# Holding five more chunks over into the next stage three of a long-convolution kernel

## The chip, the cores and the metric

The kernel runs on one core of one Trainium2 chip. The metric is the device time of one execution in microseconds (us): 1001.87 us before the change, median of 3 runs (998.74 to 1006.28).

## The reference

For a batch of 8 sequences of 6400 positions and 128 channels, the reference makes a causal long convolution and then a small gated layer:

```python
y = np.fft.irfft(np.fft.rfft(x, n=2*S, axis=1) * np.fft.rfft(h, n=2*S, axis=0)[None], n=2*S, axis=1)[:, :S]
gate_pre[:, s] = sum(conv_w[k] * y[:, s - 4 + k] for k in range(5))     # causal, 5 taps, per channel
gate = 1 / (1 + np.exp(-gate_pre))
out = (gate * (y @ w_val)) @ w_out
```

## The kernel before, in words

A position is n1 * 64 + n2, with 100 values of n1 and 64 of n2. The long convolution is done by two-step transforms, all as float32 matmuls. **Stage one** (`Forward`) transforms over n1: 16 steps of 32 short matmuls, fed by `sums`, in which GpSimd (POOL) writes the sum and the difference of the two halves of x into one of three buffers `sd`. **Stage two** (`s2_mm`, `Product`) transforms over n2 in 13 blocks `kb`: 16 matmuls `pt<-gy,m` with matrices from a ring of three buffers `m2_sb`, two multiplications on VectorE (DVE) with the filter's spectrum from a ring of four buffers `h_sb`, and two additions on GpSimd. **Stage three** (`s3_quads`) transforms back over k2 in 16 steps of 64 short matmuls `pt<-r_sb,gy`. **Stage four** (`Chunk.s4`) transforms back over k1: 20 matmuls `pt<-m_sb,dt` for a chunk of five n2; the 13 chunks are `HEAD` (60 to 63) and those that begin at 0, 5, ... 55.

The gated layer works on these chunks. `copies` puts the chunk from PSUM into `y` and starts the taps on ScalarE (ACT); `taps` adds three products per chunk on DVE (`more`, a read-modify-write of the running sum in "cells" of n2) and a fourth on GpSimd, which adds a buffer `p` that ACT had scaled. Tap j of the chunk at a adds into cells a+j to a+j+4, so neighbouring chunks write the same cells. Then come `project` (y times w_val, four matmuls of 500 columns), `sigm` on ACT, `gate` on DVE, `output` (four matmuls), and `store`.

The eight sequences b run in one software pipeline of two stretches per sequence, and every engine works strictly in the order of the program text. The **stage-three stretch** runs stage three of b with stage one of b+1, step by step: `s3_quads`, then `half` of the next sequence, then `sums` for a later `half`, then the leftover work that `steps[g]` lists. The **stage-four stretch** runs stage four of b, one chunk per step s, with stage two of b+1, one block per step. In it a chunk's taps come at step s+1, its projection at s+2, its output matmuls at s+3. For the five chunks 35 to 55 ("late") only `y` is kept; their taps, projections and outputs are left over to the next stage-three stretch, since they have storage of their own (`yl`, `gl`). The others keep `y` and cells inside `dt`, which the next stage three overwrites. The last sequence (b = 7) has no stage one or two beside it and no late chunks.

PSUM has two pairs of banks (`pair`, stages two and three) and four single banks (`single`: stage one's halves, `s4`, `project`, `output`).

Of the kernel before, what the change touches and what calls it, by code (L numbers as in the profile page):

```python
# [10 lines left out]
F32 = mybir.dt.float32  # L11
# [5 lines left out]
C = 128  # L17
N1 = 100
N2 = 64
# [5 lines left out]
SB = 4  # L25
NKB = 13
TAPS = 5
XG = 4
NS = C // (2 * XG)
NW = 2 * C + TAPS  # L30
CH = 5
HEAD = (60, 4)
# [1 line left out]
NCH = len(CHUNKS)  # L34
OUT_ORDER = CHUNKS[1:] + [HEAD]
LATE = 35
DEFER = 35
M2B = 3
MH = 6
HB = 4  # L40
XB = 3
XH = 8


def _out_range(ch):
# [76 lines left out]
def longconv_moe(ctx: ExitStack, tc: tile.TileContext, x, h, r1, m2, r3, m4, w64, out):  # L122
    nc = _Engines(tc)
    B = x.shape[0]
    MUL, ADD = ALU.mult, ALU.add

    cp = ctx.enter_context(tc.tile_pool(name="cp", bufs=1))
# [9 lines left out]
    dv = dt.rearrange("p (n c d) -> p n c d", c=2, d=C)  # L137
# [5 lines left out]
    wc_sb = w_sb[:, 2 * C :]  # L143
    gl = cp.tile([128, N2 - LATE, N1], F32, name="gl")
    yl = {a: cp.tile([128, n, N1], F32, name=f"yl_{a}") for a, n in CHUNKS if a >= LATE}
    m2_sb = [cp.tile([128, SB, 2, C], F32, name=f"m2_{i}") for i in range(M2B)]
    h_sb = [cp.tile([128, 2 * SB * C], F32, name=f"h_{i}") for i in range(HB)]
    x_sb = [cp.tile([128, 2, XG, N2], F32, name=f"x_{i}") for i in range(XB)]
    sd_sb = [cp.tile([128, 2, XG, N2], F32, name=f"sd_{i}") for i in range(3)]
    p_t = [cp.tile([128, CH, N1], F32, name=f"p_{i}") for i in range(2)]  # L150
# [118 lines left out]
    def count(kb):  # L269
        return min(SB, HR - kb * SB)  # L270
# [122 lines left out]
    def cells(x, n):  # L393

        out, i = [], 0
        while i < n:
            y = x + i
            end = 4 if y < 4 else LATE if y < LATE else N2
            k = min(n - i, end - y)
            s = (y - 4) % N2  # L400
            out.append((i, gl[:, y - LATE : y - LATE + k] if y >= LATE else dv[:, s : s + k, 1, :N1]))
            i += k
        return out

    class Chunk:


        def __init__(self, b, ch, defer):
            self.b, self.ch = b, ch
            a, n = ch  # L410
            self.late = defer and DEFER <= a < HEAD[0]
            self.y = yl[a][:, :n] if a >= LATE else dv[:, a : a + n, 0, :N1]

        def s4(self):
            a, n = self.ch
# [23 lines left out]
        def copies(self):  # L439
            a, n = self.ch  # L440
            if a == HEAD[0]:
                for i, o in cells(0, n):
                    nc.gpsimd.memset(o[:, :, :1], 0.0)
                    self.first(4, o[:, :, 1:], self.p[:, i : i + n, : N1 - 1])
                act(self.y, self.p)
                for i, o in cells(a, n):
                    self.first(0, o, self.p)
            else:
                act(self.y, self.p)
                if not self.late:  # L450
                    self.init()
                    self.q = p_t[a // CH % 2]
                    self.first(3, self.q, self.p)
            if self.late:
                self.p = self.y

        def init(self):
            a, n = self.ch
            for i, o in cells(a + 4, min(n, HEAD[0] - a - 4)):
                self.first(4, o, self.p[:, i : i + o.shape[1]])  # L460

        def taps(self, js=range(4)):
            a, n = self.ch
            if self.late and 0 in js:
                self.init()
                self.q = p_t[a // CH % 2]
                self.first(3, self.q, self.p)
            if a == HEAD[0]:
                for j in range(1, 4):
                    for i, o in cells(a + j, n - j):  # L470
                        self.more(j, o, self.p[:, : n - j])
                    for i, o in cells(0, j):
                        self.more(j, o[:, :, 1:], self.p[:, n - j :, : N1 - 1])
                return
            k = HEAD[0] - a - 4
            if k < n and 0 in js:
                for i, o in cells(HEAD[0], n - k):
                    self.more(4, o, self.p[:, k:])
            for j in js:
                if j < 3:  # L480
                    for i, o in cells(a + j, n):
                        self.more(j, o, self.p[:, i : i + o.shape[1]])
            if 3 not in js:
                return
            for i, o in cells(a + 3, n):
                nc.gpsimd.tensor_tensor(out=o, in0=o, in1=self.q[:, i : i + o.shape[1]], op=ADD)

        def project(self):
            n = self.ch[1]
# [37 lines left out]
        )  # L527
        for i in range(XH - XB)
    ]
# [7 lines left out]
    for g, (f, i) in enumerate(order):  # L537
        e = f.half()
# [12 lines left out]
        a = slice(CH * j, CH * j + CH + (j == 12))  # L551
        nc.sync.dma_start(m4_sb[:, a], m4.rearrange("k (n t) -> k n t", t=MW)[:, a])

    m4_rest = [12, 11, 10, 9, 4, 8, 5, 7, 6]
    sp, pr = {0: Spectrum(0)}, {}
    for kb in range(-1, NKB + 1):
        if 0 <= kb < NKB:
# [20 lines left out]
    pend = []  # L578
    for b in range(B):
        nxt = b + 1 < B  # L580


        steps = collections.defaultdict(list)
        for m, c in enumerate(pend[1:]):
            steps[2 * m] += [lambda c=c: c.taps(range(2))]
            steps[2 * m + 1] += [lambda c=c: c.taps(range(2, 4))]
            steps[2 * m + 2] += [c.project, c.sigm, c.gate]
            if m < 3:
                steps[2 * m + 4] += [c.output]
                steps[2 * m + 5] += [c.store]  # L590
        if pend:
            steps[13] += [pend[0].project, pend[0].sigm, pend[0].gate]
        if nxt:
            for _ in range(2):
                fx.sums(nc.gpsimd)
        for g in range(NS):
            e = s3_quads(4 * g)
            f = []
            if nxt:
                f = fx.half([single(), single()])  # L600
                fx.sums(nc.gpsimd)
            for u in e:
                u()
            for u in f:
                u(act)
            if b == 0:
                next(wgen, None)
                next(wgen, None)
                if g % 3 == 0 and g < 12:
                    m4_load(m4_rest.pop(0))  # L610
            if nxt and g % 2 and g > 1:
                kb = g // 2 - 1
                if kb < M2B:
                    m2_load(kb)
                elif kb < M2B + HB - 1:
                    h_load(kb - M2B)
            for u in steps[g]:
                u()
        if nxt:
            h_load(HB - 1)  # L620
        if b + 2 < B:
            fx = Forward(x[b + 2], gy)


        cs = [Chunk(b, ch, nxt) for ch in CHUNKS]
        jobs = collections.defaultdict(list)
        for i, c in enumerate(cs):
            if i and not c.late:
                jobs[i + 2 if nxt else (5, 6, 7, 8, 9, 10, 11, 11, 12, 13, 13, 14)[i - 1]].append(c)
        if not nxt:  # L630
            jobs[NCH + 1].append(cs[0])
        ps, outs = {}, []
        for s in range(max(NCH - 1, *jobs) + 2):
            if s < 2:
                cs[s].s4()
            if s == 0 and pend:
                pend[0].output()
                pend[0].store(p_t[1][:, : HEAD[1]])
            if nxt and s == 0:
                ps[0] = Product(0)  # L640
                m2_load(M2B)
            if nxt and s + 1 < NKB:
                ps[s + 1] = Product(s + 1)
                m2_load(s + 1 + M2B)
# [6 lines left out]
            late = pend[4 + s : 5 + s] if s < 2 else []  # L651
            for c in outs + late:
                c.output()
            for c in jobs[s]:
                c.sigm()
            if s < NCH:
                cs[s].copies()
            for c in outs + late:
                c.store()
            if s in ps:  # L660
                ps[s].mul_u()
                ps[s].mul_t()
                ps.pop(s).add()
                h_load(s + HB)
# [7 lines left out]
        pend = [cs[0]] + [c for c in cs if c.late]  # L672


def _lay_x(v):
# [42 lines left out]
```

## Time and profile before

| | |
|---|---|
| runs | 1006.28, 1001.87, 998.74 us; median 1001.87 |
| profiled execution | 1004.56 us, of which the span from the first to the last instruction is 1002.7 |
| busy share of the span | PE 87%, PEld 72%, DVE 74%, POOL 57%, ACT 51% |
| granted TensorE clock | 0.954 (mean) |
| stretches | start 97.6 us; seven cycles of a stage-three stretch (53.1 to 56.5 us) and a stage-four stretch (57.8 to 60.8 us); last sequence 42.6 and 60.4 us |
| DMA | 177.40 MB, mean 177 GB/s |

How it is read: PE is TensorE's matmuls, PEld its weight loads, which run beside them, SP the queue that issues DMAs. "Busy" is the time in which an engine has an instruction in work; `x40` is a number of instructions; the part in brackets is the idle time before, and who ended it. Every instruction bears the line of one helper (L109), so groups are told apart by their tiles: `out<-in`. A window's bounds are microseconds from the span's start.

### The profile page before, as it was taken

Reading aid. Unit: us, or ns where it says so; the run is one execution under the profiler, and the core shown is the slowest. Engines: PE = TensorE matmul, PEld = TensorE weight load, DVE = VectorE, ACT = ScalarE, POOL = GpSimd, SP = SyncE. Lnnn points to the kernel's source line nnn. Section 1 sums busy time; section 2 is a strip of 40 time slices with the busy share of each in tenths; the row PEclk is TensorE's granted clock in tenths of the full one; section 3 lists DMA queues with packets and bytes.
Section 4 is the critical chain, followed back from the end, with each engine's and each line's share of the span. In section 5 each row is a group of like instructions: output and inputs, shape, how many; then the busy total and the mean of one; then the engine's idle time right before and its main releaser. Section 6 shows DMA issues by size and latency. Waiting matters only on the chain. (4 is left out here: it accounts for less than half of the span.)

```text
span 1002.7 us, 47817 instructions
## 1 busy us (share of the span) xinstructions
PE 871.8 (87%) x21360; PEld 719.6 (72%) x21360; DVE 745.1 (74%) x1033; ACT 509.6 (51%) x1207; POOL 570.1 (57%) x586
## 2 busy tenths in 40 slices
PE   7898769988799879988899778988799888997778
PEld 6798668775688558775788657876688757884554
DVE  5556547968598767968499675968589675978666
ACT  4431444546553654547444663546544574545456
POOL 5457535775477754786277663776367762761032
PEclk9799879999999989999899999999899999999999
DMA  7684647846486456855486565855478454850103
GB/s 255 229 304 190 192 141 258 262 107 185 154 264 185 144 160 213 231 135 164 142 264 183 141 197 162 242 157 162 134 240 222 139 170 138 266 144 23 42 22 111
DMA packets 96844, 177.40 MB, mean 177 GB/s; under 512 B 43392, under 2 KB 49792, under 8 KB 96640
## 3 DMA queue, kind: packets, MB, share of 16 engines
q1 hardware_dynamic: 96640, 174.35, 56.2%
q8 instruction: 168, 2.75, 1.1%
q14 instruction: 36, 0.29, 0.1%
HBM read 141.56 MB, written 32.77 MB: 174 GB/s over the span
## 5 line engine op out<-in xcount | busy, mean ns | idle before, releaser
L109 POOL TENSOR_TENSOR gy<-gy,h 128x512 f32<-128x512 f32 (+1 forms) x182 | 221.2, 1242 | 120.1 <-PE pt L109 87.5
L109 PEld LDWEIGHTS pt<-r_sb,gy 64*64 64x64 f32 x8192 | 157.1, 145 | 103.6 <-issue 60.6
L109 DVE TENSOR_TENSOR dt<-pt,h 128x496 f32<-128x496 f32 x256 | 159.7, 664 | 96.2 <-ACT dt L109 91.8
L109 PEld LDWEIGHTS pt<-m_sb,dt 128*64 128x64 f32 x4096 | 194.0, 139 | 51.2 <-issue 34.2
L109 PE MATMUL pt<-r_sb,gy 64*64 64x64 f32 x8192 | 173.6, 233 | 60.1 <-issue 45.2
L109 PE MATMUL pt<-m_sb,dt 128*64 128x100 f32 x4096 | 200.2, 253 | 14.5 <-DVE dt L109 13.0
L109 POOL TENSOR_TENSOR sd<-x 128x256 f32<-128x256 f32 x236 | 182.0, 803 | 47.1 <-issue 21.2
L109 PEld LDWEIGHTS pt<-gy,m 128*64 128x64 f32 x3008 | 179.8, 135 | 27.7 <-issue 22.8
L109 PE MATMUL pt<-r_sb,sd 50*64 50x100 f32 x4608 | 155.0, 270 | 46.0 <-issue 21.0
L109 PE MATMUL pt<-gy,m 128*64 128x128 f32 x3008 | 190.8, 277 | 0.6 <-PE pt L109 0.5
L109 PEld LDWEIGHTS pt<-r_sb,sd 50*64 50x64 f32 x4608 | 128.6, 149 | 55.1 <-issue 24.2
L109 ACT COPY dt<-pt 128x16 f32<-128x16 f32 (+3 forms) x397 | 113.8, 329 | 103.6 <-PE pt L109 103.6
L109 DVE TENSOR_TENSOR gy<-pt,h 128x1024 f32<-128x1024 f32 (+1 forms) x99 | 116.7, 1179 | 58.3 <-ACT gl L109 34.4
L109 DVE SCALAR_TENSOR_TENSOR dt<-pt,w_sb,dt 128x500 f32<-128x500 f32 (+7 forms) x216 | 132.5, 629 | 10.6 <-POOL dt L109 6.7
L109 ACT COPY gy<-pt 128x400 f32<-128x400 f32 x248 | 112.2, 512 | 42.5 <-PE pt L109 31.2
L109 ACT COPY h<-pt 128x512 f32<-128x512 f32 (+1 forms) x136 | 83.5, 614 | 91.5 <-issue 43.0
L109 POOL TENSOR_TENSOR gl<-gl,p 128x500 f32<-128x500 f32 (+1 forms) x48 | 56.8, 1183 | 114.4 <-DVE gl L109 94.0
L109 PE MATMUL pt<-dt,w_sb 128*64 128x500 f32 (+2 forms) x480 | 115.1, 555 | 2.4 <-ACT dt L109 1.8
L109 DVE SCALAR_TENSOR_TENSOR gl<-yl,w_sb,gl 128x500 f32<-128x500 f32 (+1 forms) x112 | 106.1, 953 | 13.4 <-ACT gl L109 12.1
L109 DVE TENSOR_TENSOR h<-pt,h 128x1024 f32<-128x1024 f32 (+1 forms) x91 | 107.7, 1183 | 3.1
L109 ACT COPY yl<-pt 128x500 f32<-128x500 f32 (+1 forms) x89 | 51.3, 577 | 91.8 <-PE pt L109 91.7
L109 POOL TENSOR_TENSOR dt<-dt,p 128x500 f32<-128x500 f32 (+1 forms) x64 | 66.3, 1041 | 23.2 <-PE pt L109 13.2
(44 smaller groups left out, 657.6 us busy)
## 6 DMA issues: line engine op xcount, KB each, us to landing
m<-m SPq DMA_DIRECT2D x90, 512.0 KB, 5.4
h<-hd SPq DMA_DIRECT2D x84, 512.0 KB, 5.1
x<-xl SPq DMA_DIRECT2D x118, 256.0 KB, 2.9
out<-dt SPq DMA_DIRECT2D x56, 250.0 KB, 4.4
out<-yl SPq DMA_DIRECT2D x40, 250.0 KB, 4.6
m_sb<-m SPq DMA_DIRECT2D x12, 375.0 KB, 5.9
hd<-h SPq DMA_DIRECT2D x8, 512.0 KB, 4.9
m_sb<-m SPq DMA_DIRECT2D x6, 512.0 KB, 7.2
```

Of the source, the lines that this page charges most:

```text
L109: return self._tc.keep_in_program_order(call(*args, **kwargs))
```

## The change

Five more chunks, those at 10, 15, 20, 25 and 30, are now "held" over into the next stage-three stretch, unless it is the last sequence.

- The seven buffers of `m2_sb` and `h_sb` become slices of one tile `ring`. When stage two is through with them, five slices take the held chunks' cells (`held_c`) and `y` (`held_y`).
- In the stage-four stretch the chunks come in another order: HEAD, 0, then the late 35 to 55, then 5, then the held 10 to 30. Stage two runs ahead: two blocks in an even step, one in an odd one, so that its 13 blocks end at step 8.
- The held chunks have their taps in the stage-four stretch still, but with tap 2 scaled by ACT into an `sd` buffer and added by GpSimd behind tap 3, where DVE had added it. Their projection, sigmoid and gate stand in steps 0 to 4 of the next stage-three stretch, output and store two and three steps later. The late chunks' leftover work moves from steps 0 to 10 to steps 4 to 14; four of their outputs, not three, now fit into the stretch.
- The loads of the next stage two's first blocks move to the steps in `AHEAD`, where a slice has come free. The last sequence projects each chunk two steps after its `s4`, and the last nine loads of `m4` are reordered for the new order of the chunks.

```diff
+HELD = 10
+AHEAD = {2: (1, 0), 7: (0, 0), 9: (0, 1), 10: (0, 2), 11: (1, 1), 13: (1, 2)}
...
-    m2_sb = [cp.tile([128, SB, 2, C], F32, name=f"m2_{i}") for i in range(M2B)]
-    h_sb = [cp.tile([128, 2 * SB * C], F32, name=f"h_{i}") for i in range(HB)]
+    ring = cp.tile([128, (M2B + HB) * BL], F32, name="ring")
+    held_c = ring[:, : (LATE - HELD) * N1].rearrange("p (n t) -> p n t", t=N1)
...
+        def keep(self):
+            i = self.ch[0] // CH % 2
+            self.q = {3: p_t[i]}
+            if self.held:
+                self.q[2] = sd_sb[i].rearrange("p a d n -> p (a d n)")[:, : CH * N1].rearrange("p (n t) -> p n t", t=N1)
+            for j, q in self.q.items():
+                self.first(j, q, self.p)
...
             for j in js:
-                if j < 3:
+                if j < 3 and j not in self.q:
                     for i, o in cells(a + j, n):
                         self.more(j, o, self.p[:, i : i + o.shape[1]])
...
-            for i, o in cells(a + 3, n):
-                nc.gpsimd.tensor_tensor(out=o, in0=o, in1=self.q[:, i : i + o.shape[1]], op=ADD)
+            for j, q in self.q.items():
+                for i, o in cells(a + j, n):
+                    nc.gpsimd.tensor_tensor(out=o, in0=o, in1=q[:, i : i + o.shape[1]], op=ADD)
...
+            elif c.held:
+                t = (a - HELD) // CH
+            else:
+                t = 6 + 2 * (a - LATE) // CH
+                steps[t - 2] += [lambda c=c: c.taps(range(2))]
+                steps[t - 1] += [lambda c=c: c.taps(range(2, 4))]
+            steps[t] += [c.project, c.sigm, c.gate]
+            if t + 2 < NS:
+                steps[t + 2] += [c.output]
+                steps[t + 3] += [c.store]
...
+        if nxt:
+            cs = cs[:2] + [c for c in cs if c.late] + [c for c in cs[2:] if not c.late]
         for i, c in enumerate(cs):
-            if i and not c.late:
-                jobs[i + 2 if nxt else (5, 6, 7, 8, 9, 10, 11, 11, 12, 13, 13, 14)[i - 1]].append(c)
+            if i and not c.late and not c.held:
+                jobs[i + 2].append(c)
...
         for s in range(max(NCH - 1, *jobs) + 2):
+            kbs = list(range(at, min(at + 2 - s % 2, NKB))) if nxt else []
+            at += len(kbs)
```

The rows that follow are the engines' instructions in program order around the seam between a stage-four and the next stage-three stretch. On GpSimd before (`gy<-gy,h` are stage two's additions, `dt<-dt,p` and `gl<-gl,p` the fourth tap, `sd<-x` the sums for the next `half`):

```order
L109 TENSOR_TENSOR dt<-dt,p_93 128x2x100
L109 TENSOR_TENSOR gl<-gl,p_93 128x300
L109 TENSOR_TENSOR gy<-gy,h_84 128x64x8 x2
L109 TENSOR_TENSOR gy<-gy,h_85 128x64x8 x2
L109 TENSOR_TENSOR gy<-gy,h_86 128x64x8 x2
L109 TENSOR_TENSOR gy<-gy,h_83 128x64x4 x2
L109 TENSOR_TENSOR sd_90<-x_87 128x256 x2
```

On GpSimd now (`ring<-ring,p` is tap 3 and `ring<-ring,sd` tap 2 of a held chunk; the two rows ahead of them are tap 3 of chunk 5):

```order
L111 TENSOR_TENSOR gy<-gy,ring 128x64x4 x2
L111 TENSOR_TENSOR dt<-dt,p_88 128x2x100
L111 TENSOR_TENSOR ring<-ring,p_88 128x300
L111 TENSOR_TENSOR ring<-ring,p_87 128x500
L111 TENSOR_TENSOR ring<-ring,sd_84 128x500
...
L111 TENSOR_TENSOR ring<-ring,p_87 128x200
L111 TENSOR_TENSOR gl<-gl,p_87 128x300
L111 TENSOR_TENSOR ring<-ring,sd_84 128x300
L111 TENSOR_TENSOR gl<-gl,sd_84 128x200
L111 TENSOR_TENSOR sd_84<-x_81 128x256 x2
```

The additions of stage two stood between the taps and the sums; now they are all ahead of the taps, and the tap additions of chunk 5 and of five held chunks (two full-size additions each, the last one in four pieces) stand directly ahead of the first sums. On DVE now, in the same place (`gy<-pt,ring` and `ring<-pt,ring` are stage two's multiplications of the last block, `dt<-pt,w_sb,dt` and `ring<-pt,w_sb,ring` are taps, `dt<-pt_2860,dt` is chunk 5's gate, the last row stage three's):

```order
L111 TENSOR_TENSOR gy<-pt_2786,ring 128x2x64x4
L111 TENSOR_TENSOR ring<-pt_2786,ring 128x512
L111 SCALAR_TENSOR_TENSOR dt<-pt_2795,w_sb,dt 128x5x100
...
L111 SCALAR_TENSOR_TENSOR ring<-pt_2795,w_sb,ring 128x200
L111 SCALAR_TENSOR_TENSOR ring<-pt_2824,w_sb,ring 128x500 x2
L111 TENSOR_TENSOR dt<-pt_2860,dt 128x5x100
L111 SCALAR_TENSOR_TENSOR ring<-pt_2863,w_sb,ring 128x500 x2
...
L111 SCALAR_TENSOR_TENSOR gl<-pt_2960,w_sb,gl 128x100
L111 TENSOR_TENSOR dt<-pt_3003,ring 128x124x4
```

Before, the last taps on DVE stood eight multiplications ahead of stage three's first instruction; now every multiplication of stage two is through before chunk 5's taps, and the taps of the held chunks follow one another with nothing but one gate between.

More of the change, by code (lines that the diff above doesn't have):

```diff
@@ L36 @@
 LATE = 35
-DEFER = 35
+HELD = 10
+BL = 2 * SB * C
 M2B = 3
@@ L145, in longconv_moe @@
     yl = {a: cp.tile([128, n, N1], F32, name=f"yl_{a}") for a, n in CHUNKS if a >= LATE}
-    m2_sb = [cp.tile([128, SB, 2, C], F32, name=f"m2_{i}") for i in range(M2B)]
-    h_sb = [cp.tile([128, 2 * SB * C], F32, name=f"h_{i}") for i in range(HB)]
+    ring = cp.tile([128, (M2B + HB) * BL], F32, name="ring")
+    ring_at = [ring[:, i * BL : (i + 1) * BL] for i in range(M2B + HB)]
+    m2_sb = [r.rearrange("p (s a c) -> p s a c", a=2, c=C) for r in ring_at[:M2B]]
+    h_sb = [ring_at[M2B + i] for i in (2, 0, 1, 3)]
+    held_c = ring[:, : (LATE - HELD) * N1].rearrange("p (n t) -> p n t", t=N1)
+    held_y = {
+        a: ring[:, i : i + CH * N1].rearrange("p (n t) -> p n t", t=N1)
+        for a, i in zip(range(HELD, LATE, CH), (2500, 3072, 3572, 4096, 4596))
+    }
     x_sb = [cp.tile([128, 2, XG, N2], F32, name=f"x_{i}") for i in range(XB)]
@@ L397, in cells @@
             y = x + i
-            end = 4 if y < 4 else LATE if y < LATE else N2
+            end = next(e for e in (4, HELD, LATE, N2) if y < e)
             k = min(n - i, end - y)
             s = (y - 4) % N2
-            out.append((i, gl[:, y - LATE : y - LATE + k] if y >= LATE else dv[:, s : s + k, 1, :N1]))
+            t, o = (gl, y - LATE) if y >= LATE else (held_c, y - HELD) if y >= HELD else (dv[:, :, 1, :N1], s)
+            out.append((i, t[:, o : o + k]))
             i += k
@@ L410, in __init__ @@
             a, n = ch
-            self.late = defer and DEFER <= a < HEAD[0]
-            self.y = yl[a][:, :n] if a >= LATE else dv[:, a : a + n, 0, :N1]
+            self.late = defer and LATE <= a < HEAD[0]
+            self.held = defer and HELD <= a < LATE
+            self.y = yl[a][:, :n] if a >= LATE else held_y[a] if a >= HELD else dv[:, a : a + n, 0, :N1]
         def s4(self):
@@ L451, in copies @@
                     self.init()
-                    self.q = p_t[a // CH % 2]
-                    self.first(3, self.q, self.p)
+                    self.keep()
             if self.late:
                 self.p = self.y
+        def keep(self):
[5 more added lines that the diff above has]
+                self.first(j, q, self.p)
         def init(self):
@@ L465, in taps @@
                 self.init()
-                self.q = p_t[a // CH % 2]
-                self.first(3, self.q, self.p)
+                self.keep()
             if a == HEAD[0]:
@@ L552, in m4_load @@
         nc.sync.dma_start(m4_sb[:, a], m4.rearrange("k (n t) -> k n t", t=MW)[:, a])
[L554 removed]
+    m4_rest = [12, 7, 5, 8, 4, 9, 10, 11, 6]
     sp, pr = {0: Spectrum(0)}, {}
@@ L583, in longconv_moe @@
         steps = collections.defaultdict(list)
[L584 to L592, printed above, removed]
+        for c in pend:
+            a = c.ch[0]
+            if a == HEAD[0]:
+                t = NS - 1
+            elif c.held:
[8 more added lines that the diff above has]
+                steps[t + 3] += [c.store]
+        pend = [c for c in pend if c.ch[0] in (HEAD[0], HEAD[0] - CH)]
         if nxt:
@@ L610, in longconv_moe @@
                     m4_load(m4_rest.pop(0))
[L611 to L616, printed above, removed]
+            if nxt and g in AHEAD:
+                f, kb = AHEAD[g]
+                (h_load if f else m2_load)(kb)
             for u in steps[g]:
@@ L625, in longconv_moe, with s2, times @@
         cs = [Chunk(b, ch, nxt) for ch in CHUNKS]
+        if nxt:
+            cs = cs[:2] + [c for c in cs if c.late] + [c for c in cs[2:] if not c.late]
         jobs = collections.defaultdict(list)
         for i, c in enumerate(cs):
-            if i and not c.late:
-                jobs[i + 2 if nxt else (5, 6, 7, 8, 9, 10, 11, 11, 12, 13, 13, 14)[i - 1]].append(c)
+            if i and not c.late and not c.held:
+                jobs[i + 2].append(c)
         if not nxt:
             jobs[NCH + 1].append(cs[0])
-        ps, outs = {}, []
+        pr = {}
+        def s2(kb):
+            if nxt and kb < NKB:
+                pr[kb] = Product(kb)
+                m2_load(kb + M2B)
+        def times(kb):
+            if kb in pr:
+                pr[kb].mul_u()
+                pr[kb].mul_t()
+                pr.pop(kb).add()
+                h_load(kb + HB)
+        outs, at = [], 0
         for s in range(max(NCH - 1, *jobs) + 2):
+            kbs = list(range(at, min(at + 2 - s % 2, NKB))) if nxt else []
+            at += len(kbs)
             if s < 2:
                 cs[s].s4()
[L636 to L644, printed above, removed]
+            late = pend[s : s + 1]
+            if late and s == 0:
+                late[0].output()
+                late[0].store(p_t[1][:, : HEAD[1]])
+                late = []
+            if s == 0:
+                s2(0)
+            for kb in kbs[:1]:
+                s2(kb + 1)
             if m4_rest:
@@ L650, in longconv_moe @@
                 cs[s].s4()
-            late = pend[4 + s : 5 + s] if s < 2 else []
             for c in outs + late:
@@ L655, in longconv_moe @@
                 c.sigm()
+            for kb in kbs[:1]:
+                times(kb)
+            for kb in kbs[1:]:
+                s2(kb + 1)
             if s < NCH:
@@ L659, in longconv_moe @@
                 c.store()
[L660 to L664, printed above, removed]
+            for kb in kbs[1:]:
+                times(kb)
             if 0 < s <= NCH and not cs[s - 1].late:
@@ L671, in longconv_moe @@
                 fx.load(XB)
-        pend = [cs[0]] + [c for c in cs if c.late]
+        pend = [cs[0]] + [c for c in cs if c.held or c.late]
 def _lay_x(v):
```

## The prediction

> **What bounds the kernel now.** I read the stretches first, with the busy time of each engine (length, then busy time and count of PE, PEld, DVE, ACT and POOL, granted clock, DMA share, GB/s).
>
> ```profile
> core 0: us, PE busy (x) PEld busy (x) DVE busy (x) ACT busy (x) POOL busy (x), PEclk, DMA share, GB/s
> 97.60:153.60 56.00, 38.12 (x1540) 36.58 (x1542) 30.17 (x55) 25.30 (x80) 24.10 (x33) 0.80 0.46 150
> 669.60:724.40 54.80, 42.35 (x1577) 32.99 (x1578) 37.84 (x54) 35.22 (x100) 30.90 (x37) 0.94 0.48 146
> 724.40:785.20 60.80, 60.80 (x985) 52.66 (x982) 51.19 (x66) 25.69 (x47) 40.48 (x36) 0.97 0.73 213
> 899.70:942.30 42.60, 29.04 (x1066) 20.27 (x1066) 33.66 (x54) 21.92 (x68) 6.24 (x5) 1.00 0.06 21
> 942.30:1002.70 60.40, 50.67 (x632) 32.17 (x628) 37.22 (x62) 36.76 (x70) 15.46 (x15) 0.94 0.22 68
> ```
>
> The stage-four stretch (724.4) is PE's: it is busy for all of 60.8 us. The stage-three stretches are nobody's: no engine is busy for 80% of them. The first one (97.6) has no leftover work at all and yet takes 56.0 us, against 54.8 with five late chunks. What holds it up there:
>
> ```profile
> PE pt L109 <- issue: 15.4, 8, 3.7
> 790.11 0.81 PE L109 MATMUL pt<-r_sb,gy 64*64 64x64 f32 x41
> 791.98 0.53 PE L109 MATMUL pt<-r_sb,gy 64*64 64x64 f32 x20 [1.06 <-issue]
> q8 instruction: 168, 2.75, 1.1%
> ```
>
> PE stops 8 times for 15.4 us in the first such stretch (first row) without waiting for another engine, also in the middle of 64 like matmuls (second and third). The last row gives a reason: instructions come by DMA, 2.75 MB in 168 packets, some 16 KB each. A stage-three stretch has 1577 + 1578 = 3155 PE instructions in 54.8 us, a stage-four stretch 1967 in 60.8. So I take it that stage three goes at the pace of instruction supply, and that 500-column matmuls, few instructions with much work, cost little there.
>
> For the pace inside the stage-four stretch and at its seam I read PE's timeline.
>
> ```profile
> 724.21 2.79 PE L109 MATMUL pt<-m_sb,dt 128*64 128x100 f32 x32 [1.56 <-DVE dt L109]
> 731.62 1.05 PE L109 MATMUL pt<-gl,w_sb 128*64 128x500 f32 x4
> 771.05 2.07 PE L109 MATMUL pt<-gy,m 128*64 128x128 f32 x32
> 772.91 1.05 PE L109 MATMUL pt<-dt,w_sb 128*64 128x500 f32 x4
> 773.74 1.93 PE L109 MATMUL pt<-m_sb,dt 128*64 128x100 f32 x40
> 775.47 1.05 PE L109 MATMUL pt<-dt,w_sb 128*64 128x500 f32 x4
> 785.20 1.19 PE L109 MATMUL pt<-r_sb,gy 64*64 64x64 f32 x64
> 787.72 0.92 PE L109 MATMUL pt<-r_sb,sd 50*64 50x100 f32 x32 [1.34 <-POOL sd L109]
> ```
>
> From start to start, a stage-two block takes PE 1.86 us, a projection or output 0.83, a chunk's `s4` 1.73. From HEAD's `s4` (724.21) to the first `half` of the next stretch (787.72) are 63.5 us; this `half` waits for GpSimd's first sums.
>
> **What PE saves.** Five projections and six outputs (five held, one late) leave each of the seven stage-four stretches: 11 x 0.83 = 9.1 us of PE, all of it on the path. The same 9.1 us enter the next stretch.
>
> **The front of the stage-four stretch.** From 724.21 to 731.62, HEAD's `s4`, its output and two blocks, 7.4 us, stay as they are. Up to chunk 5's `s4` follow 10.5 blocks (19.5 us), seven `s4` (12.1) and three projections or outputs (2.5): 41.5. Only two pairs of banks serve stage two, so the third block waits for the first block's multiplications: 0.9 more, 42.4.
>
> ```profile
> 766.88 0.67 DVE L109 TENSOR_TENSOR dt<-pt,dt 128x500 f32<-128x500 f32 x1
> 767.47 1.21 DVE L109 TENSOR_TENSOR gy<-pt,h 128x1024 f32<-128x1024 f32 x1
> 768.72 1.23 DVE L109 TENSOR_TENSOR h<-pt,h 128x1024 f32<-128x1024 f32 x1
> 769.86 1.40 DVE L109 SCALAR_TENSOR_TENSOR dt<-pt,w_sb,dt 128x500 f32<-128x500 f32 x2
> 771.17 0.31 DVE L109 SCALAR_TENSOR_TENSOR gl<-pt,w_sb,gl 128x100 f32<-128x100 f32 x1
> 771.40 0.52 DVE L109 SCALAR_TENSOR_TENSOR dt<-pt,w_sb,dt 128x300 f32<-128x300 f32 x1
> ```
>
> A block's two multiplications take DVE 767.47 to 769.86, 2.39 us; three blocks in two steps are 7.2 us of it beside 9.0 of PE (three blocks, two `s4`), so PE leads this part. DMA is the one that could break it: a block needs a matrix and a spectrum of 512 KB each.
>
> ```profile
> 60.00:64.00 4.00, 4.00 (x74) 4.00 (x72) 2.36 (x2) 1.24 (x2) 2.83 (x3) 1.00 0.99 379
> m<-m SPq DMA_DIRECT2D x90, 512.0 KB, 5.4
> ```
>
> The start of the kernel shows 379 GB/s at a share of 0.99. Seven buffers are full at the stretch's start, and the other 18 loads, 9.4 MB, take 25 us of the front's 42. A matrix is asked for when its slice comes free, about 7 us ahead of its use, and lands after 5.4. It fits narrowly: nothing to 3 us, I take 1.
>
> **The tail, which decides.** Chunk 5 and the held chunks come last, and no multiplication of stage two is left to lie between their taps. The last sequence's stage four shows now what taps cost when they follow one another; the chain that ended last has there:
>
> ```profile
> 956.60 1.26 POOL dt L109
> 957.86 0.02 issue
> 957.88 0.75 DVE dt L109
> 958.64 0.02 issue
> ...
> 959.43 0.75 DVE dt L109
> 960.18 0.02 issue
> 960.21 0.04 POOLq L109
> 960.25 0.09 issue
> 960.34 1.26 POOL dt L109
> ```
>
> Three taps on DVE, one addition on GpSimd, and the next chunk's taps only then: both write the same cells (tap 3 of the chunk at a reaches cell a+7, the next chunk's tap 0 begins at a+5). A held chunk has two DVE taps of 0.77 and two GpSimd additions, and its tap 2 reaches cell a+6, so the next chunk waits for both: 1.54 + 0.15 + 1.26 + 0.1 (an estimate, from the issue row) + 1.26 = 4.3 us. The additions' pieces, and the sums behind them:
>
> ```profile
> L109 POOL TENSOR_TENSOR sd<-x 128x256 f32<-128x256 f32 x236 | 182.0, 803 | 47.1 <-issue 21.2 <-DMA x<-xl 11.0 <-PE pt L109 9.1
> L109 POOL TENSOR_TENSOR gl<-gl,p 128x300 f32<-128x300 f32 x8 | 6.6, 830 | 0.0
> L109 POOL TENSOR_TENSOR dt<-dt,p 128x200 f32<-128x200 f32 x8 | 4.9, 613 | 2.3 <-PE pt L109 2.3
> ```
>
> Counted from HEAD's `s4`: chunk 5's taps start at 43.9 (42.4, and 1.5 for ACT's first copies and DVE's last block, an estimate) and take 2.4 in five pieces; GpSimd adds 0.15 + 0.61 + 0.1 + 0.83 = 1.7, which gives 48.0. Four held chunks at 4.3: 65.2. The fifth, split at cell 35: 1.6 on DVE, 3.2 on GpSimd: 70.0. The first sums, 2 x 0.80 and an issue: 71.7; with DMA 72.7. GpSimd works in program order, so the next stretch's first `half` starts there, 9.2 us later than the 63.5 of now. PE is through with the fifth held `s4` and the first 64 stage-three matmuls at about 56 and waits some 15 us. Its 9.1 us are saved and given back with as much again.
>
> Queued behind that `half` on PE is everything of the stretch: the next `s3_quads`, the held projections, hence the gates. ACT (four activations per held chunk, two more than a chunk now since tap 2 is scaled there) has 4.3 us per chunk and hides them. Taking tap 2 off DVE (0.73 each) and moving the gates (0.59) saves DVE 6.6 us that it does not lack.
>
> **The stage-three stretch.** 9.1 us of PE come in, 12.4 us of PE's idle time stand there, and the first two rows of stretches say that the 8 projections and outputs of late chunks (6.6 us) cost nothing. Bounds: 3 less (instructions fetched during the pause), 6 more (neither hidden nor free of the clock's drop after a pause); I take +1.5, nearest to those rows. The late taps at steps 4 to 14 instead of 0 to 10 have as much around them as before. On SP the first loads for stage two move to steps 2 to 13 behind the stores of the held chunks; they are needed at the stretch's end at the earliest, and x's loads land steps ahead: nothing, or what a store's wait for ACT would add to one sum.
>
> **The last sequence.** After its predecessor's tail no sums wait, but DVE's first join of stage three stands behind the held taps, ending at about 68 instead of a join at about 62: 6 us. Five gates (3 us) come into a stretch where DVE has 33.7 busy of 42.6, and the late taps move to steps that were light: nothing. The earlier projections of stage four leave the same chain of taps: nothing, at most 4 either way. Together 6, bounds 0 and 11. The new order of `m4` loads, the same bytes: nothing.
>
> **Sum.** Six seams (b = 0 to 5) x (9.2 + 1.5) = 64, and 6: 70. On the profiled 1004.56 us that is 1075; the median of the runs lies 2.7 lower, so **1072**.
>
> **Rivals.**
> - *GpSimd alone sets the tail's pace* (the next chunk's DVE taps don't wait for both additions): 2.74 per chunk, half at 65.4 with DMA 66.4, 2.9 late; 6 x 4.4 + 6 = 32, so 1031. For it: no trace shows a held chunk's taps. Against it: the chain above.
> - *The projections are not free in stage three* (6 instead of 1.5, the last sequence 8): 6 x 15.2 + 8 = 99, 1098. For it: projection steps there have DVE, ACT and POOL queued for one another.
> - *PE's count decides*: if a held chunk's pair of taps and additions cost under about 2.2 us, the tail would hide behind PE's 13 us, and the 9.1 us remain saved: 7 x 9.1 = 64 faster, 938. For it: PE is busy through the whole stretch. Against it: two additions alone are 2.5.
> - *The pause is paid back by instruction supply.* If instructions came in during the pause of 15 us for most of the stretch behind it, stage three would run at PE's own pace there: 42.35 us of busy time in 54.8, some 12 us less. A seam would be 9.2 - 12, 2.8 us shorter: 6 x -2.8 + 6 = -11, so 991. It decides if PE holds most of a stretch's instructions. Against it: at 790.9 PE already stands for an instruction, 6 us after a stretch that used few.
>
> The Trainium skill, "Runtime: NRT & Kernel Launch", section "Instruction fetch mechanics", speaks for the last rival: it gives PE room for 2048 instructions, refilled in blocks of 256, and holds that fetching is hidden. The trace disagrees by its 15.4 us of PE stops, and by the one at 790.9; by the page the time would be the 991.
>
> **How the numbers follow.** The main case has 0.60 (1050 to 1090 by the bounds of its terms), GpSimd alone 0.12, projections not free 0.15, PE's count 0.07, instruction supply 0.06. The range takes in the first three: 1025 to 1100. Faster by over 1%: PE's count and most of the supply case, 0.11; within 1% (about what this kernel's runs can tell from no change): 0.04; slower: 0.85.
>
> **What would show it.** PE waits "POOL sd" six times for 12 to 18 us at the head of a stage-three stretch; stage four's PE is no longer busy all through, and its blocks end about 40 us after HEAD's `s4`; POOL and DVE alternate at 4.3 us per held chunk; stage three from the first `half` on keeps its 50 to 54 us. I am wrong if the wait for sums stays under 5 us, if the taps run closer, or if matrices arrive late and stretch the front.

## The result, and the profile after

The changed kernel takes 1090.02 us, median of 4 runs (1086.75 to 1096.81), against 1001.5 (998.74 to 1006.28, 4 runs): a ratio of 1.0887, 95% interval 1.0819 to 1.0955. The forecast was 1072 (1025 to 1100), slower. The profiled execution took 1088.8, its span 1087.0.

The windows of the profile after, for the last full cycle (stage four, then stage three), b = 6's stage four and the last sequence, answer to the stretches shown before:

```profile
core 0: us, PE busy (x) PEld busy (x) DVE busy (x) ACT busy (x) POOL busy (x), PEclk, DMA share, GB/s
790.60:846.10 55.50, 51.28 (x944) 47.38 (x941) 41.05 (x51) 19.88 (x38) 38.56 (x35) 1.00 0.61 204
846.10:916.70 70.60, 51.09 (x1622) 34.17 (x1622) 44.94 (x66) 43.04 (x117) 39.07 (x46) 0.88 0.45 136
916.70:971.90 55.20, 51.18 (x940) 47.29 (x937) 41.01 (x51) 19.77 (x38) 38.48 (x35) 1.00 0.62 205
971.90:1029.10 57.20, 40.34 (x1112) 23.38 (x1111) 41.19 (x66) 30.02 (x85) 14.69 (x14) 0.91 0.11 39
1029.10:1087.00 57.90, 49.06 (x628) 30.75 (x624) 37.59 (x65) 36.67 (x70) 15.60 (x16) 0.96 0.20 71
```

The stage-four stretch is 4 to 5 us shorter and PE is no longer busy all through. The stage-three stretch is 70.6 us instead of 55, at a granted clock of 0.88 instead of 0.94. Here is what PE did around the seam, from HEAD's `s4` to step 3 of stage three (a row counts 32 matmuls for a block of stage two and 40 for a chunk's `s4`, twice the calls of the program text):

```profile
790.43 1.59 PE L111 MATMUL pt<-m_sb,dt 128*64 128x100 f32 x32 [0.73 <-DVE dt L111]
...
846.07 1.19 PE L111 MATMUL pt<-r_sb,gy 64*64 64x64 f32 x64
861.38 1.61 PE L111 MATMUL pt<-r_sb,sd 50*64 50x100 f32 x32 [14.12 <-POOL sd L111]
862.92 1.93 PE L111 MATMUL pt<-ring,w_sb 128*64 128x500 f32 x4
864.78 1.99 PE L111 MATMUL pt<-r_sb,gy 64*64 64x64 f32 x64
866.55 1.28 PE L111 MATMUL pt<-r_sb,sd 50*64 50x100 f32 x32
867.76 1.06 PE L111 MATMUL pt<-ring,w_sb 128*64 128x500 f32 x4
868.75 1.19 PE L111 MATMUL pt<-r_sb,gy 64*64 64x64 f32 x64
869.76 0.87 PE L111 MATMUL pt<-r_sb,sd 50*64 50x100 f32 x32
870.56 1.90 PE L111 MATMUL pt<-ring,w_sb 128*64 128x500 f32 x8
872.39 1.19 PE L111 MATMUL pt<-r_sb,gy 64*64 64x64 f32 x64
```

From 790.43 to the first `half` at 861.38 are 70.95 us (69.7 to 71.0 at the six seams, mean 70.2). PE is through with stage three's first step at 847 and stands for 14.1 us, released by GpSimd's sums. The list of waits (us in all, times, the longest) has 84.9 us of this, nearly all of it in the six seams (13.8 to 14.1 us each), and beside it the two engines that wait for one another:

```profile
DVE ring L111 <- POOL ring L111: 85.2, 39, 3.0
PE pt L111 <- POOL sd L111: 84.9, 7, 14.1
POOL ring L111 <- DVE ring L111: 45.8, 25, 3.1
```

And the timelines of DVE and GpSimd in that tail (start, duration, number of like instructions):

```profile
834.60 1.41 DVE L111 SCALAR_TENSOR_TENSOR dt<-pt,w_sb,dt 128x500 f32<-128x500 f32 x2 [1.57 <-ACT p L111]
...
842.54 1.51 DVE L111 SCALAR_TENSOR_TENSOR ring<-pt,w_sb,ring 128x500 f32<-128x500 f32 x2 [2.17 <-POOL ring L111]
846.80 1.51 DVE L111 SCALAR_TENSOR_TENSOR ring<-pt,w_sb,ring 128x500 f32<-128x500 f32 x2 [2.75 <-POOL ring L111]
851.34 1.51 DVE L111 SCALAR_TENSOR_TENSOR ring<-pt,w_sb,ring 128x500 f32<-128x500 f32 x2 [3.02 <-POOL ring L111]
```
```profile
844.19 1.25 POOL L111 TENSOR_TENSOR ring<-ring,p 128x500 f32<-128x500 f32 x1 [1.68 <-ACT dt L111]
845.52 1.25 POOL L111 TENSOR_TENSOR ring<-ring,sd 128x500 f32<-128x500 f32 x1
848.75 1.24 POOL L111 TENSOR_TENSOR ring<-ring,p 128x500 f32<-128x500 f32 x1 [1.98 <-ACT gl L111]
...
859.23 0.61 POOL L111 TENSOR_TENSOR gl<-gl,sd 128x200 f32<-128x200 f32 x1
859.92 5.52 POOL L111 TENSOR_TENSOR sd<-x 128x256 f32<-128x256 f32 x8
```

Read across: DVE's taps end at 844.05, GpSimd's first addition starts at 844.19, its second ends at 846.77, DVE's next taps start at 846.80. Neither engine is busy all the time, and neither can go on without the other. (GpSimd's row at 844.19 names ScalarE; the addition starts 0.14 us behind the taps that write the same cells.)

### The profile page after: what moved, and what is told of

Same layout as the page of the kernel before. It is cut to its first block, busy times and chain, and to the rows that moved or that the text cites. A ratio compares the mean times of both kernels' runs of the same rounds, so it can differ in the third digit from the quotient of the medians.

```text
span 1087.0 us, 47988 instructions
## 1 busy us (share of the span) xinstructions
PE 875.4 (81%) x21360; PEld 702.5 (65%) x21360; DVE 719.4 (66%) x1007; ACT 525.8 (48%) x1250; POOL 608.1 (56%) x636
## 5 line engine op out<-in xcount | busy, mean ns | idle before, releaser
L111 POOL TENSOR_TENSOR gy<-gy,ring 128x512 f32<-128x512 f32 (+1 forms) x182 | 220.3, 1242 | 121.4 <-DVE ring L111 80.8
L111 PE MATMUL pt<-r_sb,sd 50*64 50x100 f32 x4608 | 147.9, 266 | 115.5 <-POOL sd L111 84.9
L111 DVE TENSOR_TENSOR dt<-pt,ring 128x496 f32<-128x496 f32 x256 | 160.1, 666 | 79.1 <-ACT dt L111 79.0
L111 PE MATMUL pt<-gy,ring 128*64 128x128 f32 x3008 | 189.0, 278 | 9.7 <-PE pt L111 6.0
L111 ACT COPY ring<-pt 128x512 f32<-128x512 f32 (+2 forms) x216 | 129.0, 602 | 131.1 <-PE pt L111 73.1
L111 PEld LDWEIGHTS pt<-gy,ring 128*64 128x64 f32 x3008 | 176.2, 135 | 18.8 <-PE pt L111 14.9
L111 DVE TENSOR_TENSOR ring<-pt,ring 128x1024 f32<-128x1024 f32 (+2 forms) x131 | 134.8, 1029 | 54.6 <-PE pt L111 44.2
L111 DVE TENSOR_TENSOR gy<-pt,ring 128x1024 f32<-128x1024 f32 (+1 forms) x99 | 116.8, 1180 | 63.9 <-PE pt L111 60.3
L111 DVE SCALAR_TENSOR_TENSOR ring<-pt,w_sb,ring 128x500 f32<-128x500 f32 (+2 forms) x101 | 67.6, 669 | 88.2 <-POOL ring L111 85.2
L111 POOL TENSOR_TENSOR ring<-ring,p 128x500 f32<-128x500 f32 (+2 forms) x48 | 51.3, 1070 | 71.3 <-DVE ring L111 45.8
L111 PE MATMUL pt<-ring,w_sb 128*64 128x500 f32 x320 | 86.4, 643 | 1.7 <-DVE ring L111 1.3
```

The costliest lines, as they stand in the source:

```text
L111: return self._tc.keep_in_program_order(call(*args, **kwargs))
```

## The experiments

"Half" is below the time from HEAD's `s4` to the first `half` of the next stretch, "rest" the time from there to the end of that stage-three stretch, both as means over the six seams (the end is taken some 0.2 us behind the next HEAD's `s4`, in all runs alike). Before: half 62.6, rest 52.1; after: 70.2 and 57.4. The kernel before ran beside each group: medians 1003.75, 1002.77 and 1000.49. My theory was the alternation of DVE and GpSimd over shared cells, with the sums queued behind; the rivals were GpSimd's own count of additions, and a cost of the leftover work in stage three.

**Tap 2 back on DVE.** One edit, run twice:

```diff
-            if self.held:
-                self.q[2] = sd_sb[i].rearrange("p a d n -> p (a d n)")[:, : CH * N1].rearrange("p (n t) -> p n t", t=N1)
```

> The changed kernel, with tap 2 of the held chunks back on DVE (no second scaling on ACT, no second addition on GpSimd). Theory A (DVE and GpSimd alternate over the shared cells): a held chunk costs 3 x 0.75 + 0.15 + 1.26, 3.7 us instead of 4.3, so the wait for sums shrinks from 14 to about 11 us and the time by 6 x 3 + 3 = 21 us to about 1068. Theory B (GpSimd alone sets the pace): the tail halves, the wait for sums shrinks by 6 us or more, time about 1045.

The first time gave 1059.92 and 1078.35 us, too far apart to decide by. So it ran again:

> The changed kernel with tap 2 of the held chunks added by DVE as before, once more, for a time of its own. Its trace showed the held chunks every 3.70 us in place of 4.26, and the first half of the next stretch 67.1 us after HEAD's s4 in place of 70.0: six times 2.9 is 17 less than the changed kernel's 1090, so 1073 by the chain of taps alone. If tap 2 on GpSimd and ScalarE also costs something elsewhere (the clock's drop after the longer pause, ScalarE's fifth scaling), less than that: 1055 to 1068.

1070.42 us (1068.8 to 1071.45, 4 runs), ratio 1.0706 (1.0664 to 1.0749); half 66.8, rest 57.9. Its tail, from the timelines of DVE and GpSimd, and its wait for the sums:

```profile
826.74 2.29 DVE L111 SCALAR_TENSOR_TENSOR ring<-pt,w_sb,ring 128x500 f32<-128x500 f32 x3 [0.83 <-POOL ring L111]
830.44 2.29 DVE L111 SCALAR_TENSOR_TENSOR ring<-pt,w_sb,ring 128x500 f32<-128x500 f32 x3 [1.41 <-POOL ring L111]
```
```profile
829.16 1.25 POOL L111 TENSOR_TENSOR ring<-ring,p 128x500 f32<-128x500 f32 x1 [2.46 <-ACT dt L111]
832.87 1.24 POOL L111 TENSOR_TENSOR ring<-ring,p 128x500 f32<-128x500 f32 x1 [2.46 <-DVE ring L111]
```
```profile
PE pt L111 <- POOL sd L111: 59.1, 6, 11.2
```

A chunk every 3.70 us, and 3.70 is 2.29 + 0.13 + 1.25 + 0.03: the sum of both engines, not the larger of them. Halving GpSimd's additions wins 0.56 per chunk, 3.4 at each half, and 6 x 3.4 is about the 20 us that the kernel is faster than the changed one. GpSimd's own count is refuted.

**The first sums ahead of the tail's end.** The first two sums follow the first and second held chunk's additions instead of the fifth's; x is loaded two steps earlier, and tap 2's product goes to a free slice of the ring, since the sums need the `sd` buffers.

```diff
-        if nxt:
+        if nxt and b == 0:
             for _ in range(2):
                 fx.sums(nc.gpsimd)
...
+            if s in (9, 10) and b + 2 < B:
+                fx.sums(nc.gpsimd)
```

> The changed kernel, with the first two sums of the next stage one placed behind the additions of the first and of the second held chunk instead of behind the last; x is loaded two steps earlier for it, and tap 2's scratch lies in a free slice of the ring, since the sums now take the sd buffers. The taps and their order are untouched. If the order on GpSimd makes PE's wait: the wait for sums goes (first half about 57 us after HEAD's s4 instead of 70), PE waits at step 2 instead for DVE's join behind the held taps (at about 68), and a seam gets some 6 us shorter: about 1050. If the sums were held up by something else (x, PE): no change, 1089.

1050.79 us (2 runs), ratio 1.05 (1.0411 to 1.0589). Half falls to 56.3, but rest grows to 64.7: the timeline of PE has, right behind the first `half`,

```profile
821.08 1.94 PE L111 MATMUL pt<-ring,w_sb 128*64 128x500 f32 x4 [3.43 <-DVE ring L111]
```

The same tail now holds up the held projections and the joins on DVE. A wait that is taken away at one consumer reappears at the next while the chain itself stays.

**The held chunks' taps left out**, on DVE and GpSimd both (so their gates are formed from the wrong sum): `taps` returns at once for a held chunk.

> The changed kernel without the held chunks' tap additions, on DVE and on GpSimd (ACT's scalings, the projections and all else stay): it shows what is left without the chain. First half at PE's own pace, about 57 us after HEAD's s4 against 70 now and 62.4 before. The stage-three stretch from the first half on took 57.4 us in the changed kernel against 52.1 before. Theory P (the pause does it, by a lower clock or what is queued up): back to about 52, total 1089 - 6 x 13 - 6 x 5 - 7 = about 974. Theory Q (the eleven projections and outputs do it): stays at 57, total about 1004.

1006.56 us (8 runs), ratio 1.0049 (1.0012 to 1.0086), near the second case. Half 58.4, rest 57.8. Without the tail, 84 of the 88 us are gone, but rest is as long as in the changed kernel, so the held taps and the long pause are not needed for that. A shorter pause remains at the seam, from GpSimd's wait for x:

```profile
788.77 1.61 PE L111 MATMUL pt<-r_sb,sd 50*64 50x100 f32 x32 [4.88 <-POOL sd L111]
```
```profile
POOL sd L111 <- DMA x<-xl: 41.7, 10, 10.4
```

**The addition one chunk behind.** Tap 2 on DVE, the sums early, and each held chunk's addition on GpSimd issued after the *next* chunk's taps on DVE, so that the two engines could overlap:

```diff
+            if skew and s <= NCH:
+                cs[s - 1].taps(range(3))
+                if cs[s - 2].held:
+                    cs[s - 2].taps([3])
```

> The changed kernel with three edits: tap 2 back on DVE, the first two sums behind the first two held chunks, and each held chunk's GpSimd addition placed behind the next chunk's DVE taps, so that DVE and GpSimd work on different cells at a time. Theory A: DVE then runs the held taps at 2.3 us a chunk, is through at about 59 us after HEAD's s4, and PE hardly waits: first half at about 57. With the stage-three stretch at 52 (theory P) about 975, at 57 (theory Q) about 1005, so about as fast as the kernel before or a little faster. If GpSimd's additions are the limit in themselves (theory B), the same, since there are half as many.

1040.56 us (1034.2 to 1043.06, 5 runs), ratio 1.0396 (1.0329 to 1.0464): a miss by at least 35. The timelines of DVE and ACT and the list of waits say why:

```profile
798.11 2.29 DVE L111 SCALAR_TENSOR_TENSOR ring<-pt,w_sb,ring 128x500 f32<-128x500 f32 x3 [2.13 <-ACT p L111]
802.54 2.28 DVE L111 SCALAR_TENSOR_TENSOR ring<-pt,w_sb,ring 128x500 f32<-128x500 f32 x3 [2.14 <-ACT p L111]
```
```profile
797.40 0.68 ACT L111 ACTIVATE p<-pt,w_sb 128x500 f32<-128x500 f32 x1 [3.99 <-POOL ring L111]
```
```profile
ACT p L111 <- POOL ring L111: 61.3, 21, 4.0
```

A chunk still takes 4.4 us. The chain now runs through the two buffers `p`: ScalarE must not write one before GpSimd has read it, and GpSimd reads it a chunk later than before. I had counted engines and cells, not the buffers between them.

**A scratch buffer for each held chunk.** The same, with the third to fifth held chunk's products in free places (two in the ring, one in `sd`):

```diff
+            m = (self.ch[0] - HELD) // CH
+            if self.held and m > 1:
+                o = [ring[:, 5 * BL : 5 * BL + CH * N1], ring[:, 5 * BL + CH * N1 : 5 * BL + 2 * CH * N1]]
```

> The kernel of e5 (tap 2 on DVE, sums between the first held chunks, each GpSimd addition behind the next chunk's DVE taps) with a scratch buffer of its own for each held chunk's scaled tap 3. In e5 DVE still took 4.4 us a held chunk, since ACT waited to write tap 3's scratch until GpSimd had read it two chunks earlier. Theory S (two scratch buffers close the ring DVE - GpSimd - ACT): DVE now runs the held taps at 2.3 us a chunk, PE reaches step 1 of the stage-three stretch about 59 us after HEAD's s4 instead of 63 in e5, time about 1000 (the stage-three stretch from step 1 on still 54 us). If DVE's pace had another cause: 1035 to 1040 as e5.

998.35 us (994.12 to 1004.81, 12 runs), ratio 0.9966 (0.9939 to 0.9993): the changed kernel's whole loss is gone, and 0.3% more. DVE's taps run without a break and PE reaches its first `half` 55.3 us after HEAD's `s4` at 720.82:

```profile
770.48 8.65 DVE L111 SCALAR_TENSOR_TENSOR ring<-pt,w_sb,ring 128x500 f32<-128x500 f32 x11
```
```profile
720.82 1.59 PE L111 MATMUL pt<-m_sb,dt 128*64 128x100 f32 x32 [0.78 <-DVE dt L111]
...
776.14 0.87 PE L111 MATMUL pt<-r_sb,sd 50*64 50x100 f32 x32
```

Half is 55.9, 6.7 less than before. But rest is 57.5, 5.4 more. That leaves 1.3 us a seam of the 9.1 us of PE that were moved.

**The order alone.** The changed kernel with nothing held (`self.held = False`), so five chunks are finished in the stage-four stretch as before, but behind all of stage two; the storage, the loads and the last sequence stay as changed:

> One part of the change alone: the new order of chunks and stage two running ahead, but no chunk held (10 to 30 are projected in the stage-four stretch as before the change, tap 2 on DVE). Theory A: the bare taps of six chunks at the end of the stretch cost by themselves, 3.7 us a chunk, and the projection and output of the last chunk come behind them: first half about 71 us after HEAD's s4, against 62.4 before; the stage-three stretch stays at 52 from there. 1004.6 + 6 x 9 + 6, about 1065. Theory H (holding is what costs, through the second GpSimd addition and the leftover work): about 1005.

1054.34 us (2 runs), ratio 1.052 (1.0463 to 1.0577); half 68.6, rest 53.2; between the two forecasts, nearer to the first. The new order by itself makes 52 of the 88 us. As differences of medians, holding adds 16 (1070 with tap 2 on DVE), and tap 2 on GpSimd 20. DVE's timeline has the tail, with a gate between any two chunks:

```profile
810.74 2.29 DVE L111 SCALAR_TENSOR_TENSOR ring<-pt,w_sb,ring 128x500 f32<-128x500 f32 x3 [0.84 <-POOL ring L111]
812.94 0.67 DVE L111 TENSOR_TENSOR ring<-pt,ring 128x500 f32<-128x500 f32 x1
814.85 2.29 DVE L111 SCALAR_TENSOR_TENSOR ring<-pt,w_sb,ring 128x500 f32<-128x500 f32 x3 [1.24 <-ACT p L111]
```

**The leftover work left out.** The kernel with five scratch buffers without the held chunks' projection, sigmoid, gate and output (their `y` is stored as it is):

> The kernel of e6, with the held chunks' projection, sigmoid, gate and output left out (y is stored as it is): the stage-three stretch without the work that the change moves into it. Theory Q (the moved work lengthens that stretch): from step 1 to its end about 51.5 us, as before the change, against 54 with it; with the last sequence some 25 us less than e6, about 975. Theory P (it costs nothing beside the instruction supply): as e6.

996.57 us (992.57 to 999.87, 8 runs), ratio 0.9945 (0.991 to 0.998): 1.8 us less than with them. One stage-three stretch with the leftover work, and the same one without (of the six without, it is the longest):

```profile
775.00:833.00 58.00, 51.40 (x1630) 33.56 (x1627) 45.25 (x68) 41.96 (x115) 32.97 (x39) 0.97 0.47 148
```
```profile
770.40:830.40 60.00, 46.28 (x1581) 34.98 (x1582) 40.35 (x62) 37.07 (x105) 30.26 (x37) 0.86 0.45 142
```

and PE's stops for nothing that the profile names, from the waits in these windows, with and without:

```profile
PE pt L111 <- issue: 3.4, 3, 2.0
```
```profile
PE pt L111 <- issue: 9.2, 4, 3.6
```

PE is busy 5 us less and gets no earlier to the end: it stops for longer, and its clock is 0.86. Over the six seams rest is 56.5 without the work and 57.5 with it, at a mean granted clock of 0.90 and 0.985. So the run shows that leaving the work out wins next to nothing as the kernel stands. It does not show that the work is free: the clock was not the same.

**Three held chunks instead of five** (`HELD = 20`, chunks 10 and 15 finished in stage four):

> The kernel of e6 with three chunks held (20, 25, 30) instead of five; 10 and 15 are projected in the stage-four stretch. PE gets 4 x 0.83 = 3.3 us back into the stage-four stretch and out of the next; chunks 5, 10 and 15 have their GpSimd addition between their DVE taps again (3.7 us each). If five held chunks are better only by PE's count: stage four 3 us longer, stage three 1 us shorter, about 6 x 2 us slower than e6, 1012. If the leftover work is what hurts: faster than e6.

1013.38 us (2 runs), ratio 1.0111 (1.0055 to 1.0167): half 60.9, rest 54.6. The two chunks that stay lengthen stage four by 5.0 and shorten stage three by 2.9, so once the tail is broken holding five is better than holding three, by about 1 us per chunk and seam. The total is as forecast (1012), but both terms were forecast smaller (3 and 1). How much of the 5.0 is PE's work isn't shown, since chunks 10 and 15 also have their GpSimd additions between the taps again.

**The leftover work one step later.** To see whether rest is long because the held projections come while the last taps still run:

```diff
-                t = (a - HELD) // CH
+                t = (a - HELD) // CH + 1
```

> The kernel with five scratch buffers, and the held chunks' projections, sigmoids and gates one step later (steps 1 to 5 of the next stage-three stretch in place of 0 to 4), the loads into their slices one step later too. In the kernel with five scratch buffers the stretch from its first half to its end takes 57.5 us (mean of b = 1 to 6), 4 more than in the kernel that holds nothing (53.3), and the difference is made in the first three steps (step 3 reached at 11.6 us against 6.1 to 8.9), where the last held taps still run on DVE until 5 us after the stretch's start and a gate stands between them and stage three's joins. Theory L (the projections stand too early, where they wait for those taps): a step later frees the first steps, 2 to 4 us per stretch, 12 to 24 over six: 974 to 986. Theory C (PE's own count and the instructions' supply set the stretch; the steps with a projection and an output take 3.5 us wherever they stand): within 5 us of the kernel with five scratch buffers, 993 to 1003.

1003.56 us (993.64 to 1010.59, 12 runs), ratio 1.0016 (0.998 to 1.0051): no gain; half 56.3, rest 58.4. The place of the leftover work isn't what lengthens the stretch. What does stays open: rest is 53.2 with neither held taps nor leftover work at the seam (the order alone), 54.6 with three held chunks and 57.5 with five, but also 57.8 with the leftover work and no held taps, and 56.5 with the held taps and no leftover work. Either alone comes with a long stretch, and no run has separated the two from the clock.

## Why the prediction was right, and where its terms were off

All times from HEAD's `s4` at the seam shown, unless a mean is given:

| step | forecast | measured |
|---|---|---|
| chunk 5's taps start | 43.9 | 44.2 |
| one held chunk | 4.3 | 4.2 to 4.6 |
| tail ends | 70.0 | 69.4 |
| first `half` | 72.7 | 71.0 (mean of six 70.2) |
| the same before | 63.5 | mean 62.6 |
| longer per seam | 9.2 | 7.6 |
| PE's wait | 12 to 18, six times | 13.8 to 14.1, six times |
| rest of the stretch | +1.5 (-3 to 6) | +5.3 |
| last sequence | +6 (0 to 11) | +8.1 |
| sum on the profiled execution | +70 | +84.2 |

The direction and the mechanism at the seam were right. That the time fell inside the range owes something to chance: it lies at the upper end of the main case's 1050 to 1090, the seam was forecast too long and the rest of the stretch too short. One of the signs named in advance failed: stage three from the first `half` on was to keep its 50 to 54 us, and took 55.1 to 58.3.

- **The tail** was right as a mechanism, shown by the rows of the alternation, by tap 2 on DVE (3.70 per chunk) and by the five scratch buffers, which take the alternation away and the long wait with it (half 55.9).
- **The base of the seam** was too long: I took 63.5 from one cycle, and the six lie between 61.6 and 63.7. Here is a short one of the kernel before, 61.7:

```profile
265.24 1.59 PE L109 MATMUL pt<-m_sb,dt 128*64 128x100 f32 x32 [1.57 <-DVE dt L109]
...
326.96 0.92 PE L109 MATMUL pt<-r_sb,sd 50*64 50x100 f32 x32 [1.23 <-POOL sd L109]
```

  That hid an error the other way: the 1.0 that I gave to DMA, and 0.6 of the tail's end, didn't come. The seam is 1.6 less than forecast, 10 us over six.
- **The rest of the stretch** is the term that was mis-sized: +1.5 forecast, +5.3 measured, inside its bounds. The step that failed is that the 9.1 us of projections and outputs would nearly all lie in PE's idle time. Here is the stretch from the first `half` on, at the last seam: before, after, and with five scratch buffers.

```profile
787.72:840.35 52.63, 42.11 (x1508) 31.20 (x1509) 37.16 (x54) 33.94 (x96) 29.55 (x35) 0.94 0.48 143
```
```profile
861.38:916.51 55.13, 49.74 (x1552) 32.96 (x1553) 39.04 (x57) 38.94 (x107) 29.27 (x35) 0.95 0.53 160
```
```profile
776.14:832.65 56.51, 49.91 (x1565) 32.20 (x1557) 43.93 (x66) 40.56 (x112) 31.83 (x38) 0.97 0.48 152
```

  As means of the six, PE's busy time grows from 41.1 to 50.6 us and its idle time shrinks from 10.8 to 6.7: some 4 of the 9.5 us found a place, and the stretch grew by the rest. The reading behind the +1.5 compared a stretch without leftover work with one that had it, but the first ran at a clock of 0.80 and the second at 0.94, so it could not show that the work was free.

  The clock does fall behind the pause, which I had put into the upper bound only. In PE's rows above, start to start, the first `half` takes 1.54, its projection 1.86, the 64 matmuls 1.77, the next `half` 1.21; the same at 868.75 and later take 0.80, 0.91 (1.83 for two), 1.01 and 0.80. That is 2.9 us at this seam, the longest of the six: half the clock was granted for 3.3 to 6.0 us behind the restarts, 4.7 in the mean, which costs about 2.3. It isn't shown to be the difference. Over the whole six stretches the granted clock is 0.94 before and 0.94 after, and the kernel with five scratch buffers, with no such pause and a clock of 0.985, has the same long rest (57.5). Why not more than 4 us could be hidden stays open.
- **The last sequence**: stage three 57.2 instead of 42.6, b = 6's stage four 55.2 instead of 59.2, the last stage four 57.9 instead of 60.4: 8.1. That it is near the 6 is in part chance. DVE's first join comes 66.2 us behind HEAD's `s4` instead of 61.4, 4.8 later where 6 was forecast; the stretch behind it is 5.8 longer and the last stage four 2.5 shorter, where nothing was forecast for either.
- **The sum**: 6 x (7.6 + 5.3) + 8.1 = 85.5, less 1.3 at the start, is the 84.2 that the profiled execution is longer. The forecast's error of 18 us is the rest of the stretch (6 x 3.8 = 23), the seam (-10), the last sequence and the start (together 1), and 4 for the medians: the changed kernel's lies 1.2 above its profiled execution, where I took 2.7 below.

The rivals: two of their sums took the 2.7 us between profiled execution and median off twice. On the median 1001.87, *GpSimd alone* gives 1034 and *projections not free* 1101, the second just outside the range that was to hold it. *GpSimd alone* fell with the first experiment. *Projections not free* came out in its size: it had 6 a stretch and 8 for the last sequence, measured are 5.3 and 8.1. Its cause, projection steps in which three engines queue for one another, isn't shown: moving the projections a step later won nothing. *PE's count* (938) is what the five scratch buffers come nearest to, and they gave 998: with the tail hidden, the first `half` does come 6.7 us earlier, and the rest of stage three takes 5.4 of them back. *Instruction supply paying back the pause* (991) fell by its size: the stretch behind the pause became longer, not 12 us shorter. DMA's queues, in the 15 us of the pause and in the 55 us behind it:

```profile
q8 instruction: 1, 0.02, 0.4%
```
```profile
q8 instruction: 12, 0.20, 1.6%
```

```profile
q8 instruction: 13, 0.21, 1.5%
```

One packet in the pause, then 12, against 13 in the same whole stretch before (last row). From the first `half` on, PE's stops with no releaser fall from 7.6 us a stretch to 5.1, and to 5.2 with five scratch buffers, where there is no such pause; so what the pause brought in is at most 2.5 us of the 12. Whether PE held as many instructions as it can when the pause began, no row shows.

That these stops are waits for instructions, which I had only argued, the trace before bears out: in its seven stage-three stretches beside a stage one, all 46 of them end 1.2 to 1.6 us behind the end of one of the 16 KB packets on this queue, while the packets there come some 4.5 us apart. The rule that I weighed there, the Trainium skill's "Runtime: NRT & Kernel Launch", section "Instruction fetch mechanics" (the next page is fetched while the current one runs, so that fetching is mostly hidden), isn't borne out by this trace: in the first of these stretches the stops are 15.4 of 56.0 us.

## What to carry to other kernels

When work is reordered so that an engine's read-modify-writes follow one another, look at which other engine writes the same cells: the pace becomes the sum of both engines' times, though neither is busy all the time, and whatever is queued behind on either of them waits. To break such a chain, count the buffers between the engines as well as the order: the skewed order alone left 4.4 us per chunk, and with a buffer for each chunk the taps followed one another without a break. And work moved from a stretch where PE is the bound to one with idle PE is only won in so far as the second stretch does not grow: here 6.7 us left one side and 5.4 came back on the other. When two stretches are compared to price such work, look at their clocks first.

## What the runs showed of the hardware

- PE ran at half speed behind a pause: after 14.1 us, 32 matmuls took 1.54 us instead of 0.80. The granted clock is 0.50 from 850.4 to 867.4, so full speed was back only 6.0 us after the restart, though the next matmuls followed closely; at the other five seams it took 3.3 to 5.2 us. Pauses of 4.88 and 3.43 us did the same (1.61 for 32, 1.94 for four projections). The Trainium skill, "TensorE: Matmul & The Clock Gate", Part 1, has a half-rate default that full rate replaces after a busy window of about 3.4 us that doesn't start with the work; 3.3 to 6.0 us is within two such windows, so the trace agrees.
- A lighter load for PE came with a lower clock: without the held projections the granted clock of a whole execution was 0.927 to 0.943 (eight runs), with them 0.962 to 0.976 (twelve), and the time was within 0.2%.
- PE's stops in streams of short matmuls ended 1.2 to 1.6 us behind an instruction packet (46 of 46, above). On that queue no two packets started less than 3.3 us apart, in the kernel before as after.
- A hand-over between DVE and GpSimd is short: 0.14 us from the taps' end to the addition, 0.03 us back. The alternation's cost is the durations, not the semaphores.
